# Where the weight sums of a seven-product matrix product are made: two groups of four blocks, or block by block

## The chip, the cores and the metric

The kernel runs on one core of a Trainium2 chip. The metric is device time in microseconds (us) of one launch. In the profile the core's engines are PE (TensorE, matrix products; PEld is its weight load), DVE (VectorE), ACT (ScalarE), POOL (GpSimd) and SP (SyncE, which only issues transfers here). Each engine works through its own instructions in the order in which they were written.

## The reference

An mLSTM cell makes an activation `x` of 3072 rows and 320 columns, and a feed-forward block with the gate h·cos(h) follows. Cut to what matters here:

```python
for t in range(S):                      # B, H, S, D = 4, 8, 768, 40
    ...                                 # stabilised gates, state C and n
    y[:, :, t] = o * h_tilde / denom
x = y.transpose(0, 2, 1, 3).reshape(B * S, H * D)
h = x @ w_in                            # 320 x 2048
g = h * np.cos(h)
return g @ w_out                        # 2048 x 320
```

The weights `w_in` and `w_out` arrive as 64-bit floats and are brought to 32 bits on the chip.

## The kernel before

The sequence is cut into NC = 6 chunks of 128 steps. A cell is one chunk of one batch entry, numbered n = c·4 + b, so there are 24 cells. The feed-forward work of chunk c (512 rows, all four batch entries) is cut into eight slots, f2 = 0 to 7. Slot f2 multiplies the chunk by two 128-column blocks of `w_in` ("up", tile `pup`, lines 636 and 639), applies the gate (ACT L644, DVE L647, ACT L652, DVE L656, tile `g`), and feeds the product with `w_out`.

The work is written out by hand. `both_parts(c, b)` emits slots f2 = 2b (i = 0, "even") and 2b + 1 (i = 1, "odd") of chunk c, and between their parts the cell n = (c + 1)·4 + b, which belongs to the next chunk. So two slots and one cell make a pair, and four pairs a chunk. In an even slot the cell's scores (PE L482), weighted values (`vt`, PE L508 to L517) and state increments (`pu`, PE L597) stand behind the up products, then its normalisation on DVE (L526 to L537) and one product on POOL (`yt`, L538). In an odd slot `seam_out` issues two transfers of `yt` from ACT's queue (L604), ahead of the sine of that slot (L652), and `state` (DVE L619) adds `pu` to a state that `fade` (POOL L580) has multiplied before. The up tiles have two buffers in PSUM, so the up products of a slot start when the gate of the slot before (L656) has read its buffers.

The chunk c = 0 uses the plain product with `w_out` (`down`, `po`, L668), while the last blocks of the weights are still being converted (`to_float32`, whose last step is POOL L162). From c = 1 on the product has a seven-product form. A pair of 128-row blocks of `w_out` (k = 0 to 7) and a pair of batch entries are taken as 2 x 2 blocks, and sums of them are multiplied:

- `sums(c, k)` makes the sums of the gated activations, four on DVE (L705 to L708, tile `S`) and four on POOL (L710 to L713, tiles `D`, `S` and, in place, `g`).
- `weight_sums` makes the sums of the weights once for all later chunks: `T2`, `T3` and `T4` in tile `T`, and `T1` in place of the block B12 of `w_out_sb`. All four are POOL instructions (L692 to L695). The last two read what the second has written.
- `products(c, k)` yields the matrix products for block pair k (PE L746). In chunk 1 there are twelve for each k; for X0 they read B11, B21 and then `T2`, for Y0 `T3`, `T4` and `T1`. The products of block pair k run in slot k + 1 (those of k = 7 in slot 0 of the next chunk), by `down_slot`. In slot 0 of chunk 1 `down_slot` still does the last plain product.

`weight_sums(0)`, for k = 0 to 3, is called at the end of the last slot of chunk 0, and `weight_sums(1)`, for k = 4 to 7, in slot 0 of chunk 1 behind the last plain product. Each POOL instruction of a group spans 4 x 160 columns. On POOL the first group stands between the last L162 and the next cell's mask (L391, `decay_exponents`), and the second between the activation sums of slot 0 and `yt` (L538) and `fade` (L580) of that slot's cell.

Of the kernel before, what the change touches and what calls it, by code (L numbers as in the profile page):

```python
# [29 lines left out]
def kernel(  # L30
# [30 lines left out]
    NF = DFF // 128  # L61
# [267 lines left out]
    def load_two(n, which="qkKv"):  # L329
        c, b = divmod(n, B)  # L330
        m = n // 2 % 2
        for name, src in (("q", q), ("k", k)):
            if name in which:
                src = src.rearrange("b (p j) (c t a) d -> j c t (b p) (a d)", j=2, a=C // 32, t=32)
                for j in range(2):
                    for low in range(1 if n < 2 * B else 2):
                        x = 0 if low else 32
                        dst = raws[name][m][64 * j + 32 * low:64 * j + 32 * low + 32, x:x + WR]
                        nc.sync.dma_start(out=dst.rearrange("t (p x) -> t p x", x=C // 32 * D),
                                          in_=src[j, c, :, 4 * b:4 * b + 8])  # L340
        for name, dst, src in (("K", ks2[m], k), ("v", vs2[m], v)):
            if name in which:
                src = src.rearrange("b h (c t) d -> c t b h d", t=C)
                nc.sync.dma_start(out=dst[:, :, :, 0:D], in_=src[c, :, b:b + 2])
# [34 lines left out]
    def psum_o():  # L379
        return ps_o.tile([128, HP, C], FP, name="pm", tag="o")  # L380
# [57 lines left out]
    def clear_low():  # L438
        for w in "qk":
            nc.gpsimd.memset(raws[w][1], 0.0)  # L440
# [34 lines left out]
    def scores(n):  # L475
        pool, tag = psum(n)
        qT, kT = qkT[n]
        ps = [pool.tile([128, HP, C], FP, name="ps", tag=tag) for _ in range(2)]
        for p in range(HP):
            for j in range(2):  # L480
                r = slice(64 * j, 64 * j + D)
                nc.tensor.matmul(ps[j][:, p], kT[r, p], qT[r, p], start=True, stop=True)  # L482
        pss[n] = ps
# [76 lines left out]
    def halves(n):  # L560
        for j in range(2):
            r = slice(64 * j, 64 * j + D)
            for lo, hi, x in ((0, 32, HP * 32 * j), (32, DV, H * 32)):
                s = st[n % B][r, x:x + HP * 32].rearrange("q (p d) -> q p d", p=HP)
                yield j, r, s if lo == 0 else s[:, :, 16 * j:16 * j + 16], slice(lo, hi)
# [8 lines left out]
    def fade(n):  # L574

        if B <= n < N - B:
            c, b = divmod(n, B)
            for j, r, s, w in halves(n):
                d = tab[r, c, 3, ts(b, H)].rearrange("p (a j) -> p a j", j=2)[:, :, j]
                nc.gpsimd.tensor_tensor(out=s, in0=s, in1=d.unsqueeze(2).to_broadcast([D, HP, w.stop - w.start]), op=OP.mult)  # L580
# [100 lines left out]
    def out_to(c, b, o):  # L681
        nc.sync.dma_start(out=out[b * S + c * C:b * S + (c + 1) * C], in_=o)

    def weight_sums(part):

        if part == 0:
            for i in range(3):
                T[i] = pc.tile([128, NF // 2, HALF], FP, name=f"T{i}", tag="bits")
        r = ts(part, NF // 4)
        B11, B12, B21, B22 = (wv[:, r, e, h] for e in range(2) for h in range(2))  # L690
        T2, T3, T4 = (t[:, r] for t in T)
        nc.gpsimd.tensor_tensor(out=T3, in0=B22, in1=B12, op=OP.subtract)  # L692
        nc.gpsimd.tensor_tensor(out=B12, in0=B12, in1=B11, op=OP.subtract)
        nc.gpsimd.tensor_tensor(out=T2, in0=B22, in1=B12, op=OP.subtract)
        nc.gpsimd.tensor_tensor(out=T4, in0=B21, in1=T2, op=OP.subtract)  # L695

    def sums(c, k):

        if k % 4 == 0:
            Ds[c, k // 4] = pb.tile([128, 4, 2, C], FP, name="D", tag="bits")  # L700
        D1, D4 = (Ds[c, k // 4][:, k % 4, i] for i in range(2))
        S = Ss[c, k] = p2.tile([128, 4, C], FP, name="S", tag="S")
        G0, G1 = (gs[c, 2 * k + e].rearrange("q (p e t) -> q p e t", p=2, e=2) for e in range(2))
        tt = nc.vector.tensor_tensor
        tt(out=S[:, 2], in0=G0[:, 0, 1], in1=G1[:, 0, 1], op=OP.add)  # L705
        tt(out=S[:, 0], in0=S[:, 2], in1=G0[:, 0, 0], op=OP.subtract)
        tt(out=S[:, 3], in0=G1[:, 0, 0], in1=S[:, 0], op=OP.subtract)
        tt(out=G0[:, 0, 1], in0=G0[:, 0, 0], in1=G0[:, 0, 1], op=OP.subtract)  # L708
        tt = nc.gpsimd.tensor_tensor
        tt(out=D1, in0=G0[:, 1, 1], in1=G1[:, 1, 1], op=OP.add)  # L710
        tt(out=S[:, 1], in0=D1, in1=G0[:, 1, 0], op=OP.subtract)
        tt(out=D4, in0=G1[:, 1, 0], in1=S[:, 1], op=OP.subtract)
        tt(out=G0[:, 1, 1], in0=G0[:, 1, 0], in1=G0[:, 1, 1], op=OP.subtract)  # L713

    LAST = NF // 2 - 1
# [96 lines left out]
    def warm(k, bank=None):  # L812

        for _ in range(k):
            nc.tensor.matmul(bank or pw, nil, nil.unsqueeze(1).to_broadcast([128, HP, 128]), start=True, stop=True)
# [130 lines left out]
    def both_parts(c, b):  # L946

        n = (c + 1) * B + b
        cell = n < N
        for i in range(2):  # L950
            f2 = 2 * b + i
            up = Up(c, f2)
            if cell and i == 0:
                scores(n)
                if c == 0 and b == 0:

                    warm(8, psum_o())
            if cell and i == 1:
                if n % 2 == 1 and n > B + 1 and n + 3 < N:
                    load_two(n + 3, "Kv")  # L960
            for e in range(2):
                up.near(e)
            for e in range(2):
                up.rest(e)
            if i == 0:
                if cell:
                    weigh(n)
                    if n + 1 < N:
                        decay_exponents(n + 1)
                    if n == B:  # L970
                        clear_low()
                for e in range(2):
                    up.sin(e)
                    up.gate(e)
                if c > 0:
                    sums(c, f2)
                if b == 0 and 0 < c < NC - 1:
                    sigmoid(c + 1)

                if c == 0 and b > 0 and pieces:  # L980
                    to_float32(*pieces.pop(0))
                if c == 0:
                    next_out()
                if cell and n + 1 < N:
                    decay(n + 1)
            else:
                if cell:
                    seam_out(n)
                if pieces:
                    to_float32(*pieces.pop(0))  # L990
                if cell:
                    state(n)
                for e in range(2):
                    up.sin(e)
                    up.gate(e)
                if c > 0:
                    sums(c, f2)
                if n == B + 1:
                    low_dimensions(n + 1)
                while pieces:  # L1000
                    to_float32(*pieces.pop(0))
                if cell and n + 1 < N:
                    weigh_k(n + 1)
                    odd_values(n + 1)
            down_slot(c, f2)
            if (c, f2) == (1, 0):
                weight_sums(1)
            if cell and i == 0:
                turn_gate(n)
                values(n)  # L1010
                seam(n)
                normalize_turned(n)
                fade(n)
                if n % 2 == 1 and n > B + 1 and n + 3 < N:
                    load_two(n + 3, "qk")
                if n > B + 1 and n + 3 < N:
                    load_E(n + 3)
                if b == B - 2 and c + 2 < NC:
                    load_o(c + 2)
                if c == 0 and pieces:  # L1020
                    to_float32(*pieces.pop(0))
                sin_next()
            if f2 == 0 and c > 1:
                for p in range(2):
                    combine(c - 1, p)
            if i == 1:
                if c == 0 and b + 2 < B:
                    pieces.extend(weights_in(b + 2))
                    load_two((n + 3) // 2 * 2)
                    load_E(n + 3)  # L1030
                if cell and n + 1 < N:
                    turn_blocks(n + 1)
                    scale_q(n + 1)
                if c == 0:
                    next_out()
                if (c, f2) == (0, LAST):
                    weight_sums(0)

    pieces, outs = [], []
    with tc.manual_schedule():  # L1040
# [38 lines left out]
```

## Time and profile before

| what | value |
|---|---|
| time, three runs | 553.79, 556.17, 556.29 us; median 556.17 |
| span of the profiled execution, first to last instruction | 549.6 us |
| mean granted clock of PE | 0.981 |
| PE busy | 522.2 us, 95% of the span |
| DVE busy | 420.0 us, 76% |
| ACT busy | 280.4 us, 51% |
| POOL busy | 235.3 us, 43% |
| POOL L692 to L695 together | 12.5 us, eight instructions of 128 x 640, 143.5 to 159.5 us |
| slots of chunk 1 | 138.0 to 222.7 us |

The profile gives the profiled execution by its span alone; the three timed runs lie 4.1 to 6.6 us above that span. Busy shares are averages over the whole program. The stage that the diff touches lasts from the end of chunk 0 to the end of chunk 1.

### The profile page before, as it was taken

How to read it: one execution, taken by the hardware profiler on the slowest of the kernel's cores; microseconds unless marked ns; L12 is line 12 of the kernel's file. 1: busy time of each engine (PE TensorE's matmuls, PEld its weight loads, DVE VectorE, ACT ScalarE, POOL GpSimd, SP SyncE). 2: the span in 40 equal slices, each digit the busy share in tenths (PEclk: the TensorE clock that was granted, in tenths of full speed). 3: DMA queues.
4: the chain of work that ended last, by engine and by line, in shares of the span. 5: the costliest groups of instructions: out<-in, count | busy, mean ns of one | idle time of the engine just before them, and what ended most of it. 6: DMA issues, size and time to landing. Idle time of an engine off the chain costs nothing.

```text
span 549.6 us, 10494 instructions
## 1 busy us (share of the span) xinstructions
PE 522.2 (95%) x3844; PEld 348.6 (63%) x3844; DVE 420.0 (76%) x906; ACT 280.4 (51%) x537; POOL 235.3 (43%) x381
## 2 busy tenths in 40 slices
PE   7997989989979999999999999999999999999996
PEld 4873554546646666756766756766756757575755
DVE  5864999997877787887886888787887878674645
ACT  2867966847455445555535555535556533231311
POOL 7535456463784545534444435444423421221211
PEclk9968899999999999999999999999999999999999
DMA  9998878687926538318438428338410000010001
GB/s 135 228 201 224 244 163 215 137 188 186 163 92 155 72 92 187 41 67 202 49 93 183 44 67 199 52 92 181 47 69 25 5 6 6 1 48 1 1 1 48
DMA packets 99939, 57.81 MB, mean 105 GB/s; under 512 B 62304, under 2 KB 92608, under 8 KB 99888
## 3 DMA queue, kind: packets, MB, share of 16 engines
q1 hardware_dynamic: 96496, 55.64, 47.2%
q10 hardware_dynamic: 3248, 1.33, 1.1%
q8 instruction: 30, 0.49, 0.4%
q14 instruction: 21, 0.17, 0.1%
q0 software_dynamic: 144, 0.18, 0.1%
HBM read 51.71 MB, written 4.11 MB: 102 GB/s over the span
## 4 chain that ended last, share of the span: by engine, by line
PE 65%; DVE 11%; ACT 9%; POOL 5%; DMA 3%; issue 3%; SPq 3%; ACTq 0%; DVEq 0%; POOLq 0%
PE pup L636 24%; PE acc L746 21%; PE pup L639 7%; PE late L746 2%; PE ps L482 2%; DVE n L647 2%; ACT E L405 2%; DVE g L656 2%; PE vt L517 2%; PE po L668 2%; PE vt L508 1%; ACT n L644 1%; DMA E<-M_d 1%; DVE st L619 1%; DVE t L455 1%
## 5 line engine op out<-in xcount | busy, mean ns | idle before, releaser
L636 PE MATMUL pup<-xT,w_in_sb 128*128 128x512 f32 x384 | 178.8, 609 | 8.2 <-DVE g L656 7.8
L644 ACT ACTIVATE n<-pup 128x512 int32<-128x512 f32 x96 | 52.2, 595 | 206.4 <-PE pup L639 206.3
L647 DVE SCALAR_TENSOR_TENSOR n<-pup,n 128x512 f32<-128x512 f32 x96 | 61.8, 686 | 91.2 <-ACT n L644 91.2
L636 PEld LDWEIGHTS pup<-xT,w_in_sb 128*128 128x128 f32 x384 | 70.6, 192 | 84.2 <-issue 61.2
L710 POOL TENSOR_TENSOR D<-g 128x128 f32<-128x128 f32 x40 | 19.8, 495 | 178.6 <-DVE g L656 156.7
L652 ACT ACTIVATE n<-n 128x512 f32<-128x512 f32 x96 | 58.5, 631 | 18.5 <-DVE n L647 14.7
L656 DVE SCALAR_TENSOR_TENSOR g<-pup,n 128x512 f32<-128x512 f32 x96 | 61.7, 685 | 2.1 <-ACT n L652 0.4
L746 PE MATMUL acc<-w_out_sb,g 128*128 128x160 f32 x320 | 59.0, 305 | 0.0
L746 PE MATMUL acc<-T,g 128*128 128x160 f32 x320 | 58.3, 302 | 0.0
L639 PE MATMUL pup<-xT,w_in_l 64*128 64x512 f32 x192 | 54.2, 641 | 0.0
L746 PEld LDWEIGHTS acc<-w_out_sb,g 128*128 128x128 f32 x320 | 47.4, 190 | 6.8 <-issue 4.5
L746 PEld LDWEIGHTS acc<-T,g 128*128 128x128 f32 x320 | 47.8, 190 | 4.4 <-issue 3.8
L405 ACT ACTIVATE E<-E,tab 128x128 f32<-128x128 f32 x160 | 49.2, 391 | 2.0 <-POOL E L391 1.7
L668 PE MATMUL po<-w_out_sb,g 128*128 128x320 f32 x128 | 36.6, 439 | 3.8 <-POOL w_out_sb L162 3.7
L639 PEld LDWEIGHTS pup<-xT,w_in_l 64*128 64x128 f32 x192 | 14.4, 184 | 36.5 <-issue 34.3
L746 PE MATMUL acc<-T,S 128*128 128x160 f32 x160 | 35.3, 302 | 0.0
L538 POOL TENSOR_TENSOR yt<-yt,db 128x128 f32<-128x128 f32 x20 | 10.9, 545 | 55.0 <-DVE db L533 55.0
L668 PEld LDWEIGHTS po<-w_out_sb,g 128*128 128x128 f32 x128 | 23.7, 190 | 16.4 <-POOL w_out_sb L162 4.5
L482 PEld LDWEIGHTS ps<-t,t 40*128 40x128 f32 x384 | 24.8, 188 | 10.9 <-issue 8.0
L488 DVE TENSOR_TENSOR E<-ps,E 128x512 f32<-128x512 f32 x48 | 30.7, 681 | 0.0
L464 POOL TENSOR_TENSOR qG<-t,G 128x512 f32<-128x512 f32 x20 | 25.7, 1285 | 10.2 <-DVE t L455 10.0
L746 PE MATMUL acc<-w_out_sb,S 128*128 128x160 f32 x160 | 29.1, 301 | 0.0
(176 smaller groups left out, 902.5 us busy)
## 6 DMA issues: line engine op xcount, KB each, us to landing
E<-M_d SPq DMA_DIRECT2D x22, 512.0 KB
qr<-in_q_dram SPq DMA_DIRECT2D x36, 160.0 KB
kr<-in_k_dram SPq DMA_DIRECT2D x36, 160.0 KB
G<-G_d SPq DMA_DIRECT2D x20, 256.0 KB
bits<-in_moe_w_out_dram SPq DMA_DIRECT2D x8, 640.0 KB
bits<-in_moe_w_in_dram SPq DMA_DIRECT2D x32, 128.0 KB
out_dram<-o_sb SPq DMA_DIRECT2D x24, 160.0 KB
ks<-in_k_dram SPq DMA_DIRECT2D x10, 320.0 KB
```

Of the source, the lines that this page charges most:

```text
L405: nc.scalar.activation(out=Es[n][:, h], in_=Es[n][:, h], func=AF.Exp, scale=-1.0, bias=tab[:, c, 0, g:g + 1])
L464: nc.gpsimd.tensor_tensor(out=qG, in0=qkT[n][0], in1=Gs[n], op=OP.mult)
L482: nc.tensor.matmul(ps[j][:, p], kT[r, p], qT[r, p], start=True, stop=True)
L488: nc.vector.tensor_tensor(out=w, in0=pss[n][j], in1=w, op=OP.mult)
L636: nc.tensor.matmul(pu, w_in_sb[:, i, ts(2 * f2 + e, 128)], x(i), start=(i == 0), stop=False)
L639: nc.tensor.matmul(pu, w_in_l[r, f2], x(NK, r), start=False, stop=True)
L644: nc.scalar.activation(out=self.n[e], in_=self.pu[e], func=AF.Copy, bias=0.25)
L647: nc.vector.scalar_tensor_tensor(out=self.n[e].bitcast(FP), in0=self.pu[e], scalar=0.25, in1=self.n[e], op0=OP.add, op1=OP.subtract)
L652: nc.scalar.activation(out=r, in_=r, func=AF.Sin, scale=TWO_PI_DOWN)
L656: nc.vector.scalar_tensor_tensor(out=g, in0=self.pu[e], scalar=TWO_PI, in1=self.n[e].bitcast(FP), op0=OP.mult, op1=OP.mult)
L668: nc.tensor.matmul(po[c][b], gs[c, f][:, ts(b, C)], w_out_sb[:, f], start=(f == 0), stop=(f == NF - 1))
L746: nc.tensor.matmul(a, lhs, rhs, start=start, stop=stop)
```

## The change

`weight_sums` takes a block pair k instead of a half, and makes the four sums of that pair alone: 160 columns to an instruction instead of 640. The two group calls go. `weight_sums(0)` is called in slot 0 of chunk 1, behind `fade`. `weight_sums(k)` for k = 1 to 7 is called in slot k of chunk 1, behind `sums(1, k)`.

```diff
-    def weight_sums(part):
-
-        if part == 0:
+    def weight_sums(k):
+
+        if k == 0:
             for i in range(3):
                 T[i] = pc.tile([128, NF // 2, HALF], FP, name=f"T{i}", tag="bits")
-        r = ts(part, NF // 4)
+        r = slice(k, k + 1)
         B11, B12, B21, B22 = (wv[:, r, e, h] for e in range(2) for h in range(2))
         T2, T3, T4 = (t[:, r] for t in T)
         nc.gpsimd.tensor_tensor(out=T3, in0=B22, in1=B12, op=OP.subtract)
         nc.gpsimd.tensor_tensor(out=B12, in0=B12, in1=B11, op=OP.subtract)
         nc.gpsimd.tensor_tensor(out=T2, in0=B22, in1=B12, op=OP.subtract)
         nc.gpsimd.tensor_tensor(out=T4, in0=B21, in1=T2, op=OP.subtract)
@@ both_parts, even slot (i == 0)
                 if c > 0:
                     sums(c, f2)
+                if c == 1 and b > 0:
+                    weight_sums(f2)
@@ both_parts, odd slot (i == 1)
                 if c > 0:
                     sums(c, f2)
+                if c == 1:
+                    weight_sums(f2)
@@ both_parts, behind the slot's products
             down_slot(c, f2)
-            if (c, f2) == (1, 0):
-                weight_sums(1)
             if cell and i == 0:
                 turn_gate(n)
                 values(n)
                 seam(n)
                 normalize_turned(n)
                 fade(n)
+                if (c, f2) == (1, 0):
+                    weight_sums(0)
@@ both_parts, end of the odd slot
                 if c == 0:
                     next_out()
-                if (c, f2) == (0, LAST):
-                    weight_sums(0)
```

## The prediction

> **What bounds the kernel now.** I read the page first, then the list of waits, the chain of waits around the groups, and last the stretches and engine timelines. The page says which engine to guard:
>
> ```profile
> PE 522.2 (95%) x3844; PEld 348.6 (63%) x3844; DVE 420.0 (76%) x906; ACT 280.4 (51%) x537; POOL 235.3 (43%) x381
> ```
>
> PE is the bound, so only a PE stall is worth anything. In the waits, one thing about the weight sums is visible at PE:
>
> ```profile
> PE pup L636 <- DVE g L656: 7.8, 6, 4.0
> ACT n L652 <- POOL st L580: 3.8, 1, 3.8
> ```
>
> Of 7.8 us that the up products waited for a gate, 4.0 is a single wait, and ACT's sine waited once, 3.8 us, behind POOL. The chain (start, us, engine, line) shows that both are one event:
>
> ```profile
> 143.55 1.53 POOL T L692
> ...
> 153.04 1.53 POOL T L692
> ...
> 159.49 0.41 POOL yt L538
> ...
> 161.10 0.64 ACT n L652
> 161.74 0.02 issue
> 161.76 0.70 DVE g L656
> 162.46 0.04 issue
> 162.51 5.40 PE pup L636 x8
> ```
>
> POOL runs without a pause from 142 (the last L162) to 161: the first group (143.5 to 150.0), the mask, the activation sums, the second group (153.0 to 159.5), then yt. Slot 1's sine stands on ACT behind the transfers of yt (L604, 159.93 to 161.05), so the sine, the gate and slot 2's up products all wait for the second group. PE had finished slot 1's products at 158.47 and stood still until 162.51. The stretches (us, then busy time of PE, PEld, DVE, ACT and POOL, then granted clock, DMA share, GB/s) add a second cost:
>
> ```profile
> 158.50:162.50 4.00, 0.00 (x0) 0.00 (x0) 1.68 (x6) 1.15 (x2) 2.67 (x6) 1.00 0.06 18
> 162.50:166.50 4.00, 3.99 (x6) 1.67 (x7) 3.90 (x7) 0.00 (x0) 3.15 (x6) 0.66 0.34 133
> 183.70:203.20 19.50, 19.39 (x160) 12.99 (x160) 15.37 (x37) 9.87 (x19) 9.32 (x17) 1.00 0.28 70
> ```
>
> After the stall the clock is granted at 0.66, and eight up products take 5.40 us where the same eight take 3.70 at 183.71. So the event costs 4.04 + 1.70 = 5.74 us. It also shows in the period: pairs start at 162.51, 183.71, 203.21 and 222.71, 21.2 us for the first and 19.5 for the others. A wait of 2.18 us at 74.2 left the clock at 1.00, so a stall well below 4 us need not bring the slow stretch.
>
> **What goes.** Both groups leave their places, 6.4 us on POOL each. Behind the last L162 (ends 143.5) the mask runs at 143.6 to 144.7 instead of 149.9, and ACT's decay exponents, which waited 1.72 us for it, need not wait. DVE gains too, by these rows, slot 0 first and an ordinary slot below:
>
> ```profile
> 147.08 1.42 DVE L705 TENSOR_TENSOR S<-g 128x128 f32<-128x128 f32 x1
> 173.40 0.29 DVE L705 TENSOR_TENSOR S<-g 128x128 f32<-128x128 f32 x1
> ```
>
> L705 to L708 took from 147.08 to 151.70 beside the first group, each ending with a POOL instruction; in the ordinary slot they take 1.49 us. The gate of slot 0 ends at 147.04 either way, so with POOL free the four end at 148.6. The turned gate ends at 149.4, and the normalisation then waits for vt, whose last product ends at 149.85 on PE: it starts at 149.9 instead of 152.3. From its start to yt on POOL an ordinary cell takes 2.73 us (175.56 to 178.29): yt at 152.65, fade from 153.2 to 154.55. ACT's transfers of yt and DVE's state no longer wait. From the end of slot 1's up products (155.0) the ordinary distance to the next up products is 3.52 us (180.19 to 183.71), so the gate allows slot 2 at 158.5.
>
> **What comes.** Eight groups of four POOL instructions of 160 columns. No row has that shape. The nearest is 128 columns: L710 to L713 start at 192.95, 193.59, 194.13 and 194.68, a step of 0.58; L692 to L695 with 640 columns step by 1.64. On the line between, which lies close to the 128-column end, a step is 0.58 + 32/512 x 1.06 = 0.65 and a duration 0.46 + 32/512 x 1.09 = 0.53. A group is 4 x 0.65 = 2.6 us (bounds 2.3 at the 128-column step, 6.6 if an instruction cost as much as one of 640 columns). POOL's work grows from 12.8 to some 20.8 us, in eight places.
>
> The Trainium skill ("Perfetto Trace Analysis", GPSIMD Engine Instruction, under the lifecycle part) advises against reported POOL durations and for start-to-start spacing. The rows bear that out mildly: a step of 0.58 against a mean duration of 0.52. By durations alone T2 below would come 0.2 us earlier, and the gain summed up below would be about 5.1 instead of 4.86.
>
> *k = 0* stands behind fade, from 154.55. Its third instruction, T2, ends at 154.55 + 2 x 0.65 + 0.53 = 156.4, T4 at 157.0. These two rows of PE matter:
>
> ```profile
> 155.59 0.43 PE L746 MATMUL acc<-T,S 128*128 128x160 f32 x2
> 155.86 0.71 PE L746 MATMUL acc<-T,g 128*128 128x160 f32 x4
> ```
>
> The first needs T2 at 155.59 and now stalls 0.8 us; T4, the second of the next four, is needed at 156.13 + 0.8 and comes about 0.1 late. PE therefore ends the twelve products at 158.47 + 0.9 = 159.35, later than the 158.5 that the gate allows. Slot 2 starts at 159.35. What is late next is thus T2 itself. The bounds of this stall are 0.6 (128-column prices) and 4.9 (640-column prices), and I take 0.9.
>
> *k = 2, 4, 6*, even slots, go between the activation sums and yt. *k = 1, 3, 5, 7*, odd slots, go between the activation sums and weigh_k, scale_q (L464) and the next mask. POOL's timeline of an ordinary pair shows the room (in brackets the idle time before):
>
> ```profile
> 188.93 1.08 POOL L391 TENSOR_SCALAR_AFFINE_SELECT E<-E 128x1024 f32<-128x1024 f32 x1
> 192.95 0.56 POOL L710 TENSOR_TENSOR D<-g 128x128 f32<-128x128 f32 x1 [2.94 <-DVE g L656]
> 197.81 0.55 POOL L538 TENSOR_TENSOR yt<-yt,db 128x128 f32<-128x128 f32 x1 [2.67 <-DVE db L533]
> ```
>
> Even slot: 2.6 us fits into 2.67. Were it longer, yt (ends 198.36) is first wanted by L604 on ACT at 199.90 and fade (ends 199.7) by DVE's state at 201.57, so 1.5 us more are covered. Odd slot: scale_q would end at 191.6 and PE first reads it at 193.2; the mask would end at 192.6, while ACT starts the decay at 192.45, 0.15 late before 3.3 us of idle ACT time. The products of block k start in the next slot (189.4 for k = 3, whose group would end by 189.1; T2 is only their third operand). I cost all seven at nothing. If the cover were gone, each pair would lose what a group exceeds 4.2 us by, twice. The new waits of PE on POOL add up to 0.05 us each by the small issue steps in the chain, at most 0.8 us; I take 0. Transfers: none is issued by the moved calls, and none waits behind POOL.
>
> The Trainium skill ("SBUF — State Buffer", Who interferes with whom) speaks against spreading: a DVE instruction with two SBUF inputs and a POOL instruction that reads SBUF exclude each other for a whole instruction. L705 above agrees (1.42 against 0.29). In the new places the rule would touch DVE L537 (197.63) in three pairs, at up to 0.6 us; if nothing covered it, 1.8 us of the gain would go. DVE then idles 2.32 us, so I take nothing off.
>
> **The sum.** Slot 2 starts 162.51 - 159.35 = 3.16 us earlier and its up products regain 1.70: 4.86 us. The later pairs keep their 19.5 us and move as a whole, since no transfer is waited for there. The profile gives no own time beside the span; a span of 549.6 - 4.9 = 544.7, with the 6.6 us between it and the median of the runs shown, is 551.3.
>
> **Rivals.**
>
> *The stall only shrinks.* T2 arrives at 157.5 or later (instructions of some 0.9 us), or the slow stretch comes in spite of a short stall. Then only about 3 us are won: 553.2. For it: the slow stretch follows PE's idle share in a stretch that I can't place exactly. Against: the 2.18 us wait without one.
>
> *Hidden anyway.* Something else holds slot 2 until about 162 (a transfer of slot 2's cell, say): 555.5 to 556.5. Against: the transfers are quiet then, DMA share 0.06, and every link of the chain from yt to PE is ordinary work.
>
> *POOL becomes the bound in chunk 1 (slower).* If short instructions cost much more than 0.65, the seven groups outgrow their room: from a group of 4.2 us on, yt is late for L604 in even slots and scale_q for PE in odd ones. Gain and loss balance near 1.1 us an instruction. At 640-column prices (6.6 us) six slots lose 2.4 us each, 14.4, against nothing won: 570. The milder end, some 1.2 us an instruction, gives 558 to 560. Against it stand all 160 rows of L710 to L713, 0.46 to 0.52 us in the mean.
>
> *The sums are not tracked block by block (does not do what it says).* If each run of products waited for the whole of T, PE would stand until the group of its own slot, some 8 us in seven slots: over 600. Against: PE read T at 155.59 while POOL was writing the other half at 156.25 to 159.5.
>
> **How the numbers follow.** Forecast 0.68; the shrunken stall 0.14; hidden 0.08; POOL bound 0.07; not tracked 0.03. About 0.5% (2.8 us) is what a measurement of this kernel can tell from no change. The shrunken stall straddles that bound, half of it counts as same, as does a tenth of the forecast's own chance: faster 0.68, same 0.22, slower 0.10. Low end: the forecast with the smaller stall (551.0) and the 2.4 us by which the shortest run shown lies under the median, 548.6. High end: the shrunken stall and the lower part of the hidden case, 555.3.
>
> **What would show it.** Right: PE's wait before slot 2's up products falls from 4.04 to at most 0.3, a wait of about 0.9 on POOL T appears before the third product of slot 1, clock 1.00 throughout chunk 1, pairs of 19.5 us, L692 to L695 at about 0.53 with 0.65 between starts, L705 in slot 0 at 0.3. Wrong: idle time of ACT before L652 behind POOL in other pairs, PE waiting for qG or T in slots 2 to 7, or a clock under 1.00 after slot 1.

## The result, and the profile after

| | before | after |
|---|---|---|
| time, first comparison (4 runs each), median and range | 556.07 us (553.79 to 556.29) | 548.45 us (546.25 to 550.21) |
| ratio, 95% interval | | 0.9884 (0.9845 to 0.9922) |
| time, second comparison, one chip (23 and 6 runs) | 554.06 us (550.85 to 556.28) | 547.55 us (546.06 to 548.62) |
| ratio, 95% interval | | 0.9878 (0.9846 to 0.9910) |
| span of the first profile | 549.6 us | 548.4 us |

The change makes the kernel 1.2% faster. Yet the two first profiles differ by 1.2 us only, because the opening, up to slot 0 of chunk 1, took 3.8 us longer in the profile after (slot 0 starts at 141.76 instead of 137.99 on PE) with the same instructions. So the stages are compared from slot 0 on. From slot 0 to slot 4 the profile before takes 45.72 us, the profile after 40.74. From the end of chunk 1 to the end of the program the two take 326.9 us each.

The page of the kernel after, and its list of waits, answer to the lines shown of before:

```profile
PE 525.9 (96%) x3844; PEld 351.9 (64%) x3844; DVE 415.8 (76%) x906; ACT 280.3 (51%) x537; POOL 239.4 (44%) x405
```

```profile
PE pup L636 <- DVE g L656: 6.5, 5, 2.6
```

POOL has 24 instructions more and 4.1 us more work. The single wait of 4.0 us is gone; the longest left, 2.6, is in the opening, at 71 us. The chain of waits (start, us, engine, line) now reaches slot 2 without POOL's groups:

```profile
158.88 0.61 ACT n L644
159.49 0.02 issue
159.51 0.70 DVE n L647
160.22 0.01 issue
160.22 3.04 PE acc L746 x20
163.27 3.43 PE pup L636 x8
```

Slot 2's up products follow slot 1's products directly. PE's timeline (idle time in brackets) shows the one wait that has come. The trace lists each of these products twice (384 records of L636 for 192 products), so x8 stands for four products and x2 for one:

```profile
160.22 0.54 PE L746 MATMUL acc<-T,S 128*128 128x160 f32 x2 [0.69 <-DVE n L647]
163.10 3.60 PE L636 MATMUL pup<-xT,w_in_sb 128*128 128x512 f32 x8
```

The view names DVE's L647, which ends at the same moment, but this product does not read what L647 writes; it reads T2. POOL's timeline says when T2 (L694) was ready: at 159.64 + 0.53 = 160.17.

```profile
156.47 0.56 POOL L538 TENSOR_TENSOR yt<-yt,db 128x128 f32<-128x128 f32 x1 [3.39 <-DVE db L533]
156.99 1.38 POOL L580 TENSOR_TENSOR st<-st,tab 40x128 f32<-40x128 f32 x4
158.44 0.52 POOL L692 TENSOR_TENSOR T<-w_out_sb 128x160 f32<-128x160 f32 x1
159.04 0.52 POOL L693 TENSOR_TENSOR w_out_sb<-w_out_sb 128x160 f32<-128x160 f32 x1
159.64 0.53 POOL L694 TENSOR_TENSOR T<-w_out_sb 128x160 f32<-128x160 f32 x1
...
177.08 0.55 POOL L538 TENSOR_TENSOR yt<-yt,db 128x128 f32<-128x128 f32 x1 [0.37 <-DVE db L533]
...
191.75 0.56 POOL L710 TENSOR_TENSOR D<-g 128x128 f32<-128x128 f32 x1 [0.64 <-DVE g L656]
```

In later slots the groups fill POOL's gaps nearly to the brim: 0.37 us is left before yt (2.67 in before) and 0.64 before the activation sums of an even slot (2.94). The stretches (us, busy time of PE, PEld, DVE, ACT, POOL, granted clock, DMA share, GB/s) show a full clock where it had been 0.66:

```profile
158.50:162.50 4.00, 3.31 (x22) 2.81 (x21) 2.92 (x8) 2.32 (x4) 2.04 (x4) 1.00 0.30 107
162.50:166.50 4.00, 4.00 (x14) 1.94 (x12) 3.78 (x7) 0.00 (x0) 3.20 (x7) 1.00 0.27 87
183.70:203.20 19.50, 19.39 (x161) 12.98 (x160) 15.37 (x37) 9.84 (x19) 13.44 (x25) 1.00 0.26 66
```

POOL has 4.1 us more work in an ordinary pair than before (13.44 against 9.32), PE has the same. And DVE's first activation sum of slot 0 is as short as in any slot:

```profile
150.85 0.29 DVE L705 TENSOR_TENSOR S<-g 128x128 f32<-128x128 f32 x1
```

### The profile page after: what moved, and what is told of

Same layout as the page of the kernel before. It is cut to its first block, busy times and chain, and to the rows that moved or that the text cites. A ratio compares the mean times of both kernels' runs of the same rounds, so it can differ in the third digit from the quotient of the medians.

```text
span 548.4 us, 10519 instructions
## 1 busy us (share of the span) xinstructions
PE 525.9 (96%) x3844; PEld 351.9 (64%) x3844; DVE 415.8 (76%) x906; ACT 280.3 (51%) x537; POOL 239.4 (44%) x405
## 3 DMA queue, kind: packets, MB, share of 16 engines
q1 hardware_dynamic: 96496, 55.64, 46.9%
## 4 chain that ended last, share of the span: by engine, by line
PE 65%; DVE 12%; ACT 7%; DMA 6%; SPq 4%; issue 3%; POOL 2%; ACTq 0%; DVEq 0%; POOLq 0%
PE pup L636 25%; PE acc L746 21%; PE pup L639 7%; DVE n L647 3%; PE late L746 2%; PE ps L482 2%; ACT E L405 2%; PE vt L517 2%; PE po L668 2%; DMA bits<-in_moe_w_in_dram 2%; PE vt L508 1%; DVE g L656 1%; DMA ks<-in_k_dram 1%; DMA vs<-in_v_dram 1%; DVE st L619 1%
## 5 line engine op out<-in xcount | busy, mean ns | idle before, releaser
L636 PE MATMUL pup<-xT,w_in_sb 128*128 128x512 f32 x384 | 178.3, 607 | 6.8 <-DVE g L656 6.5
L647 DVE SCALAR_TENSOR_TENSOR n<-pup,n 128x512 f32<-128x512 f32 x96 | 61.8, 686 | 90.3 <-ACT n L644 90.3
L636 PEld LDWEIGHTS pup<-xT,w_in_sb 128*128 128x128 f32 x384 | 70.4, 192 | 82.1 <-issue 61.0
L639 PEld LDWEIGHTS pup<-xT,w_in_l 64*128 64x128 f32 x192 | 14.4, 184 | 36.7 <-issue 33.4
```

Source lines behind the costliest of these rows:

```text
L636: nc.tensor.matmul(pu, w_in_sb[:, i, ts(2 * f2 + e, 128)], x(i), start=(i == 0), stop=False)
L639: nc.tensor.matmul(pu, w_in_l[r, f2], x(NK, r), start=False, stop=True)
L647: nc.vector.scalar_tensor_tensor(out=self.n[e].bitcast(FP), in0=self.pu[e], scalar=0.25, in1=self.n[e], op0=OP.add, op1=OP.subtract)
```

## The experiments

All runs together, times on PE from the start of slot 0 of chunk 1. "0 to 4" is the stage of the prediction, "0 to 8" is the whole of chunk 1.

| run | slot 0 starts at | 0 to 2 | 0 to 4 | 0 to 8 |
|---|---|---|---|---|
| before, three profiles | 137.99, 138.68, 137.71 | 24.52, 24.52, 24.50 | 45.72, 46.62, 46.50 | 84.72, 85.63, 85.72 |
| after, three profiles | 141.76, 138.54, 141.69 | 21.34 each | 40.74 each | 79.75 each |
| second group behind fade | 138.87 | 21.72 | 45.00 | 84.33 |
| the same, in blocks | 141.80 | 21.71 | 42.81 | 82.16 |
| both groups behind fade | 136.85 | 27.57 | 47.62 | 87.08 |
| after, groups twice as long | 139.24 | 21.32 | 40.72 | 83.46 |
| after, block 0 behind the sums | 138.64 | 20.60 | 40.10 | 79.11 |

**Both kernels again.** No edit.

> The changed kernel, unedited, timed again beside the kernel before. The stage from the start of slot 0 of chunk 1 (its first up product on PE) to the start of slot 4 took 45.72 us in the profile before and 40.74 in the profile after, 4.98 less, while the medians differ by 7.6 us. Theory: the change is worth the 4.9 to 5.0 us of that stage and nothing else, and the other 2.6 us are scatter of the opening (the first 138 us, whose instructions are the same in both kernels): time 4.5 to 5.5 us under before, ratio 0.990 to 0.992, stage 40.7. Rival: the change also shortens something outside the stage, and 7 to 8 us come again, ratio 0.986 or less.

> The kernel before, unedited, as a measure of the scatter. Theory: ratio 1.000 within 0.004; the stage from slot 0 to slot 4 of chunk 1 takes 45.7 us again, with a PE wait of about 4 us before slot 2 and a clock under 1.00 after it; the start of slot 0 on PE moves by some us against 138.0 (before) and 141.8 (after). Rival: the 4 us wait or the slow stretch is an accident of the one profile, and the stage takes 44 us or less.

> The kernel before, profiled once more. Two profiles show the wait before slot 2 at 4.04 and 4.03 us, but slot 2's first eight up products at 5.40 and 6.30 us (3.70 elsewhere). Theory: the wait is fixed and the slow stretch behind it depends on where it falls, so the wait is 4.0 again, those products take 5.0 to 7.4 us and the stage is 45.3 to 47.5. Rival: the stretch is sometimes absent, 3.7 us, stage 44.0.

> The changed kernel, profiled a third time. Theory: the stage is 40.74 again and the span is the start of slot 0 plus 79.75 plus 326.9, so any difference in time between runs of this kernel lies in the opening. Rival: the stage or what follows it varies as well, by 0.5 us or more.

The after kernel repeats its stage to 0.01 us, and its spans (548.4, 545.2, 548.3) differ by the start of slot 0 alone. The kernel before has the 4.0 us wait each time, but a slow stretch of two sizes. PE's timeline of the second profile, then of the third:

```profile
163.20 6.30 PE L636 MATMUL pup<-xT,w_in_sb 128*128 128x512 f32 x8 [4.03 <-DVE g L656]
```

```profile
162.21 6.21 PE L636 MATMUL pup<-xT,w_in_sb 128*128 128x512 f32 x8 [4.02 <-DVE g L656]
```

They take 5.40 us in the first profile, and here 2.60 and 2.51 us more than the ordinary 3.70. The stretches of the first profile, then of the second, show why: the clock stands at 0.50 for one length of time or for twice that.

```profile
160.00:163.70 3.70, 1.19 (x3) 0.67 (x4) 2.81 (x8) 1.15 (x2) 1.67 (x5) 1.00 0.27 102
163.80:167.10 3.30, 3.30 (x5) 1.33 (x4) 2.68 (x5) 0.00 (x0) 3.22 (x5) 0.50 0.23 76
```

```profile
160.00:161.50 1.50, 0.00 (x0) 0.00 (x0) 0.47 (x2) 0.00 (x0) 1.43 (x5) 1.00 0.00 0
161.70:168.40 6.70, 5.20 (x6) 2.16 (x7) 5.12 (x10) 1.15 (x2) 4.58 (x8) 0.50 0.38 128
168.60:171.00 2.40, 2.40 (x19) 1.17 (x19) 0.00 (x0) 0.35 (x1) 0.65 (x1) 1.00 1.20 211
```

Read in steps of 0.25 us, the slow stretch lasts 3.4 us in the first profile and 6.8 in the other two, where the first 1.6 and 1.8 us of it fall into the wait. Half of the slow time in which PE works is then 1.7, 2.6 and 2.5 us, which is what the products lose.

So by the profiles the change is worth 4.98, 5.88 and 5.76 us up to slot 4. On one chip the ratio 0.9878 is 6.8 us, with 5.0 to 8.5 in its interval, more than the 4.5 to 5.5 I had expected, and the interval holds the two larger stage gains. The kernel before against itself gave 0.9973 (0.9947 to 0.9999), so part of the rest is scatter. No run supports a gain outside chunk 1.

**Is it the place of the second group?** The call moves behind fade, nothing else:

```diff
-            if (c, f2) == (1, 0):
-                weight_sums(1)
             if cell and i == 0:
                 ...
                 fade(n)
+                if (c, f2) == (1, 0):
+                    weight_sums(1)
```

> Before, with one call moved: the second group (blocks 4 to 7, 640 columns to an instruction) stands behind fade in slot 0 instead of ahead of yt. The first group keeps its place. Theory (place): what cost time was the second group ahead of yt; yt then comes at about 155, slot 1's sine no longer waits, slot 2 starts 21.8 us after slot 0 (before 24.5, after 21.3), the slow stretch is gone: stage 41.0 to 41.8, 4.0 to 4.7 us under before. Rival (size): the large groups themselves are the cost, and the first one, which holds up the mask and DVE's sums, keeps most of the loss: stage 43.5 to 45.7, at most 2 us won.

Slot 2 starts 21.72 us after slot 0, as the place theory says. The 1.25 us for which PE still waits there are the first group's: yt starts 17.10 us after slot 0, and 14.71 in after, where no group stands ahead of the mask. But the stage is 45.00, the number of the rival though not for its reason: 0.7 us less than the first profile of before, and a ratio of 0.9976 (0.9949 to 1.0002). The loss has moved on. DVE's timeline in slot 1, then POOL's, then PE's:

```profile
161.49 1.52 DVE L706 TENSOR_TENSOR S<-S,g 128x128 f32<-128x128 f32 x1
163.05 1.58 DVE L707 TENSOR_TENSOR S<-g,S 128x128 f32<-128x128 f32 x1
```

```profile
161.21 1.66 POOL L694 TENSOR_TENSOR T<-w_out_sb 128x640 f32<-128x640 f32 x1
162.94 1.54 POOL L695 TENSOR_TENSOR T<-w_out_sb,T 128x640 f32<-128x640 f32 x1
```

```profile
160.59 3.70 PE L636 MATMUL pup<-xT,w_in_sb 128*128 128x512 f32 x8 [1.25 <-DVE g L656]
...
167.18 1.16 PE L482 MATMUL ps<-t,t 40*128 40x128 f32 x16 [1.83 <-DVE t L455]
```

L706 ends as POOL's L694 ends (163.0 and 162.9), L707 as L695 ends (164.6 and 164.5). The transposes L455 behind them come late and PE waits 1.83 us for the scores. Then a slow stretch follows:

```profile
165.30:167.20 1.90, 0.07 (x4) 0.05 (x2) 1.90 (x3) 1.08 (x2) 1.82 (x4) 1.00 0.01 4
167.20:169.00 1.80, 1.80 (x19) 1.68 (x20) 1.60 (x4) 1.40 (x3) 1.80 (x3) 0.86 0.99 234
169.00:173.50 4.50, 4.50 (x26) 4.33 (x29) 4.04 (x9) 4.47 (x10) 2.72 (x5) 0.68 1.16 200
```

So neither of my two theories was whole: by these rows the place decides over slot 1, and what comes behind it goes by the large instructions, be it their length or their work together. The next run tells these two apart.

**The length of one instruction, in the same place.** The moved group cut into blocks (`weight_sums` takes the slice as a second argument):

```diff
-                    weight_sums(1)
+                    for k in range(4, 8):
+                        weight_sums(1, slice(k, k + 1))
```

> The run with the second group behind fade, with that group cut into blocks: 16 instructions of 160 columns instead of four of 640, same place, same columns. It takes 9.6 us of POOL instead of 6.5. With the large instructions DVE's L706 and L707 in slot 1 took 1.52 and 1.58 us instead of 0.43 and 0.50, each ending with a POOL instruction, the transposes came late, and PE waited 1.83 us for them before the scores of slot 2. Theory (length of the single instruction): DVE's sums wait at most 0.6 us each, L455 is early enough, the 1.83 us wait goes; but scale_q is late by 3 us more, and PE waits 1 to 2.5 us for it at vt. Stage 42.6 to 44.0, against 45.0. Rival (amount of POOL work in that place): the same wait or a longer one before the scores, stage 45.5 or more.

DVE's timeline, then PE's:

```profile
164.47 0.57 DVE L706 TENSOR_TENSOR S<-S,g 128x128 f32<-128x128 f32 x1
165.08 0.56 DVE L707 TENSOR_TENSOR S<-g,S 128x128 f32<-128x128 f32 x1
```

```profile
174.36 0.43 PE L517 MATMUL vt<-qG,st 128*32 128x128 f32 x8 [1.10 <-POOL qG L464]
```

With more POOL work in the same place (9.3 us from the first start to the end of the last instruction) DVE waits less, the wait before the scores and the slow stretch are gone, and the stage is 42.81. The other cost comes forward as expected: scale_q is late, PE waits 1.10 us for it. That is what the spreading over the slots avoids.

**Both groups whole behind fade.** `weight_sums(0)` and then `weight_sums(1)` stand behind fade.

> Before, with both groups whole (640 columns) behind fade in slot 0. Theory: T2 of block 0 comes 3 instructions of 1.65 us after fade instead of 3 of 0.6, so slot 1's third product waits 3.5 to 4.0 us, T4 1.3 more, slot 2 starts 25 to 26 us after slot 0 and a slow stretch follows: stage 44.5 to 48, no better than before; that is what the small blocks buy for block 0. Rival: only the place ahead of yt matters, PE waits 1 us at most: stage 41 to 42.

```profile
158.37 0.54 PE L746 MATMUL acc<-T,S 128*128 128x160 f32 x2 [3.77 <-POOL T L694]
159.99 0.90 PE L746 MATMUL acc<-T,g 128*128 128x160 f32 x2 [0.64 <-POOL T L695]
```

PE's timeline names T2 and T4, the two waits of the prediction, at 3.77 and 0.64 us. The clock stands at 0.50 from 158.8 us on, shortly behind the first of them (two records that take 0.43 us elsewhere take 0.90), slot 2 starts at 27.57 (25 to 26 expected, without that), and the stage, 47.62, is longer than before. T4 follows T2 because the fourth instruction reads T2; only the third reads what the second has written. Made in the same place, block 0 alone costs 0.69.

**How much cover the groups have.** Blocks 2 to 7 get four instructions more each:

```diff
+        for _ in range(2 if k > 1 else 0):
+            nc.gpsimd.tensor_tensor(out=T2, in0=B22, in1=B12, op=OP.subtract)
+            nc.gpsimd.tensor_tensor(out=T4, in0=B21, in1=T2, op=OP.subtract)
```

> After, with the groups of blocks 2 to 7 twice as long: T2 and T4 are made three times over, eight instructions instead of four, same values. It adds 2.4 us of POOL to each of six slots. Theory (the cover named in the prediction): up to about 1.6 us of delay is covered by the slack of yt and scale_q, the rest shows, and the delay of an odd slot runs on into the even slot behind it: 3 to 8 us, stage 0 to 8 (79.75 in after) 82.7 to 88. Rival (fully covered): 79.75 to 80.3. Rival (POOL is already the bound): all 14.4 us show, 94.

Chunk 1 grows by 3.71 us of the 14.4 added. Slots 2 to 4 lose nothing (19.40 us, as in after), the two later pairs lose 2.53 and 1.21. PE's timeline:

```profile
186.92 0.54 PE L749 MATMUL acc<-T,S 128*128 128x160 f32 x2 [0.56 <-POOL T L697]
...
201.99 3.70 PE L636 MATMUL pup<-xT,w_in_sb 128*128 128x512 f32 x8 [1.61 <-DVE g L656]
```

The wait of 0.56 is for a second writing of T2 (L697 there), which belongs to this experiment alone. It occurs in slots 4 and 6, each of which takes 12.07 us instead of 11.18, so about 1.8 of the 3.71 us are its work. The 1.61 us is the delay of yt through ACT's queue that the prediction described: yt ends at 198.30, ACT issues its transfers (L604) from 198.33 to 200.53, and the sine starts at 200.58. So there is cover for most of 2.4 us more a group; longer groups were not tried.

**Block 0 like the others.** The call of block 0 moves from behind fade to behind the activation sums of slot 0:

```diff
-                if c == 1 and b > 0:
+                if c == 1:
                     weight_sums(f2)
...
-                if (c, f2) == (1, 0):
-                    weight_sums(0)
```

> After, with block 0 made right behind the activation sums of slot 0 (ahead of yt) like the other blocks, instead of behind fade. In the profile after, POOL idles 3.39 us there and a group takes 2.4, and PE then waits 0.69 us for T2 in slot 1. Theory: the group fits, the wait for T2 goes, slot 2 starts 3.5 us after the end of slot 1's up products instead of 4.26: stage 40.0, 0.7 us less than after, about 5.6 under before. Rival: yt comes later by the group, the gate of slot 1 takes the place of T2: stage 40.7 or more.

POOL's timeline, then PE's:

```profile
153.34 0.55 POOL L538 TENSOR_TENSOR yt<-yt,db 128x128 f32<-128x128 f32 x1 [1.08 <-DVE db L533]
```

```profile
156.25 0.43 PE L746 MATMUL acc<-T,S 128*128 128x160 f32 x2
```

The group fits into the 3.39 us, yt starts 14.70 us after slot 0 as in after (14.71), T2 is not waited for, and the stage is 40.10, 0.64 less than after. The timed ratio to before is 0.9865 (0.9833 to 0.9897), which can't be told from that of after; the profile's stage can, and by it this is the fastest version.

## Why the prediction was right, and where it was not

The mechanism held, and so did the places where the waits come and go. Measured from slot 0's start, with the forecast's own times:

| step | forecast | profile after |
|---|---|---|
| yt starts | 14.66 | 14.71 |
| T2 is ready | 18.4 | 18.41 |
| slot 2 starts | 21.36 | 21.34 |
| PE's wait for T2 and T4 | 0.9 | 0.69 |
| slot 2 to slot 4 | 19.5 | 19.40 |
| step of the 160-column instructions | 0.65 | 0.60 |
| the stage's gain | 4.86 | 4.98 against the same profile |

*The wait moves from the gate to T2.* Right. The run with block 0 behind the sums takes T2's wait away and the run with both groups whole makes it 3.77: its size follows the length of POOL's instructions.

*The seven later groups cost nothing.* Right: slots 2 to 4 take 19.40 us, and the doubled groups show that there was room to spare. What I named as a bound, 0.05 us for each new wait of PE, does not show in the stage. One reading was a little off: in before PE reads scale_q's tile first at 192.99, not 193.2, so an odd slot had 1.4 us of cover instead of 1.6.

*DVE's sums are held up by the first group.* Right: L705 of slot 0 takes 1.42 us in before and 0.29 in after. How long DVE is held goes by the single POOL instruction: L706 takes 1.52 us beside 640 columns, 0.57 beside 160 and 0.43 in an ordinary slot, where POOL's own sums of 128 columns run beside it. In the new places this cost nothing that PE saw. The Trainium skill ("SBUF — State Buffer", Who interferes with whom) says that a DVE instruction with two SBUF inputs contends with a POOL instruction that reads SBUF, over a shared port pair that is an exclusive lock. These times are in line with it.

*A short stall need not bring the slow stretch.* Right for the 0.69 us of after. As a rule of size it fell: the 1.83 us wait of the run with the second group behind fade brought one, the 2.18 us wait at 74 us in before had not. And the very wait that I leaned on, PE's for L162, took 2.19 us in the second profile of after and was followed by 3.4 us at 0.50 (76.4 to 79.8 us). PE had waited 2.6 us some seven us before it there, and 1.05 in before. So the argument from the one wait was weaker than I took it for, and that no stretch followed the 0.69 us is not a rule.

*The sum.* Two terms were mis-sized. The regained clock, 1.70 us, was that of one profile; two others show 2.60 and 2.51, so the gain is up to 0.9 us larger. And the 6.6 us that I laid around the span are not there: in every run whose time and span are both known the difference is 1.7 to 1.9 us (550.21 and 548.4, or 552.12 and 550.3). So the profile before was of an execution of some 551.4 us, shorter than the three runs that I was shown. I took a difference between executions for a fixed part of the time. With 1.8 the profile's sum would have been 546.5, which is the forecast for an opening of 138 us.

That the time came within 3 us of 551.3 is in part luck. The sum had 4.8 us too many around the span, and the openings of the four runs made up some 2 us of that: worked out from their spans, since the rest of the kernel after takes 406.6 us in all three profiles, they last 137.8 to 141.8 us. The median, 548.45, lies just under the low end of my range, 548.6; the ratio laid on the 556.17 us that I was shown gives 549.7, inside it.

The timed difference of the medians, 7.6 us in the first comparison and 6.5 in the second, is larger than the forecast 4.86. Two of the three stage differences are nearly 6, and the rest fits the scatter of the openings: taken together, the 35 executions of before on the one chip have a median span of 551.8 us and the six of after 545.8, which is 6.0 less. The opening of a single run of before can't be worked out from its span, because its stage varies too.

*The rivals.* Sums not tracked block by block, POOL as the bound, and a gain hidden by something else are excluded by the stage alone. "The stall only shrinks" did not come either. Its price was somewhat low: by the forecast's own terms T2 at 157.5 would still have won 3.7 us, not 3.

## What to carry to other kernels

Work that an in-order engine does long before it is needed can still stand ahead of something that is needed at once; look in the chain for the small instruction behind the large one (here a product of 0.45 us behind 6.4 us of sums). Moving one large group whole was worth little here (0.7 to 1.6 us against the three profiles of before), cutting both and spreading them over gaps that the timeline shows, each a little larger than a piece, was worth 5 to 6. Compare the stage that a change touches between profiles of both kernels, since spans carry the scatter of everything before it.

## What I had not expected of the hardware

The clock fell behind waits of very different length, and not always behind the same wait. A PE wait of 1.83 us, after one of 1.25 some five us earlier, brought a slow stretch. In the opening PE has two waits in all eleven profiles, one ahead of the up products at 67 to 71 us and one for L162 some four us behind these. Seven times the first takes 2.6 us: four times the slow stretch follows at once, and the second wait is then 0.5 us; twice it follows behind a second wait of 2.2 us; once, in the run with both groups behind fade, neither brings one. Four times the first takes 0.9 to 1.1 us, and the 2.2 us of the second bring none. Every slow stretch named here stood at 0.50 and lasted 3.4 or 6.8 us: 3.4 the six times in the opening and behind the 1.83 us, 3.4 once and 6.8 twice behind the 4.0 us, 6.8 in the run with both groups behind fade. What decides which it will be no run here shows.

And the opening, with the same instructions on every engine, moved the whole of the rest by up to 5.0 us from one execution to the next. Most of that arises early: in the three profiles with slot 0 at 141.7 to 141.8, one of them of a version of before, the first up products start at 46.8 to 46.9 us, in the other eight at 41.6 to 42.3. The cause was not looked for.
